# Attention weights transposed by DMA instead of TensorE, and MLP chunks as one stream of alternating first and last products

## The chip, the cores and the metric

The kernel runs on one core of one Trainium2 chip. Its time is the device time of that core in microseconds, from the first instruction to the last. Three runs of the kernel before took 1746.2, 1747.33 and 1747.04 us; the median is 1747.04.

A core has five engines that run side by side, each executing its own queue of instructions in order, with semaphores between them: TensorE (PE, matrix products; results go to PSUM, here in banks of 512 float32 per partition), VectorE (DVE), ScalarE (ACT), GpSimd (POOL) and SyncE (SP), which here issues the DMAs. Tiles have 128 partitions.

## What is computed

Top-32 attention over 8 batches of 8 heads, 576 queries and keys of 64 elements, and then a feed-forward block (MLP) over the 4608 rows of 512 that come out of it, with a hidden width of 2048:

```python
scores = scale * np.matmul(q, k.transpose(0, 1, 3, 2))
kth = np.partition(scores, -32, axis=-1)[..., -32:-31]
scores = np.where(scores >= kth, scores, -1e9)
scores = scores - np.max(scores, axis=-1, keepdims=True)
attn = np.exp(scores)
attn = attn / (np.sum(attn, axis=-1, keepdims=True) + 1e-09)
x = np.matmul(attn, v)                    # then (B,H,S,D) -> (B*S, H*D)

h = x @ w_in                              # 4608x512 @ 512x2048
g = np.where(h >= 1, h, np.where(h <= -1, 0.0, (h + 1) ** 2 / 4))
out = g @ w_out                           # 4608x2048 @ 2048x512
```

q, k and v are float32. The two weight matrices come as 64-bit floats, and the kernel makes 32-bit floats of them, from the two 32-bit words of each.

## The kernel before

A step of attention takes one tile of 128 queries and two heads; there are 144. Tokens are laid out so that 512 of the 576 keys form four blocks of 128 (`main`), and the last 64 of the two heads share a fifth (`tail`). In a step TensorE makes the scores, ScalarE evicts them from PSUM and takes exponentials, VectorE finds the 32nd largest score, GpSimd divides by the sum, TensorE transposes the attention weights (with the keys on the partitions, as the product with the values needs them), ScalarE evicts the transposed blocks, and TensorE multiplies them with the values.

`paired` is true for the run that is timed: VectorE looks for the largest among 288 pairwise maxima and corrects by the pairwise minima. A second run without that shortcut follows only if a flag says that the shortcut, or a very small weight, was not covered; the flag is also what `inspect_piece` and `judge` are for.

Weights are converted in 64 pieces of 128x256, first all of w_in, then all of w_out, by two instructions of ScalarE, one or two of VectorE and one or two of GpSimd each, during the first 12 steps:

```python
pieces_of_weights = [(w_in[:, kk, c:c + WC], moe_w_in[kk * P:(kk + 1) * P, c:c + WC])
                     for c in range(0, DFF, WC) for kk in range(NK)]
pieces_of_weights += [(w_out[:, f, c:c + WC], moe_w_out[f * P:(f + 1) * P, c:c + WC])
                      for f in range(NF) for c in range(0, DM, WC)]
```

Scores, the top-32 search (VectorE throughout), the softmax weights, their transposing and the product with the values:

```python
def scores(st):
    t, hp, kT, qT = st["t"], st["hp"], st["keys"]["kT"], st["qT"]
    st["s"] = s = att.tile([P, 2, S], F32, name="s", bufs=3)
    for hf in range(2):
        sp = [ps.tile([P, SH], F32, name="sp", tag="a", bufs=4) for _ in range(2)]
        c0, c1 = hf * SH, (hf + 1) * SH
        for i in range(2):
            for j in ([i] if t < NT else [0, 1]):
                d = slice(j * D, (j + 1) * D)
                g = hp if t < NT else hp + i
                o = sp[i] if t < NT else sp[i][j * TL:(j + 1) * TL]
                for a0, a1, k0 in pieces(i, j, c0, c1):
                    nc.tensor.matmul(o[:, a0 - c0:a1 - c0], qT[d, g, :], kT[d, g, k0:k0 + a1 - a0],
                                     start=True, stop=True)
        for i in range(2):
            nc.scalar.activation(s[:, i, c0:c1], sp[i], AF.Copy, scale=SCALE)
# ...
def pairs(st):
    s = st["s"]
    st["more"] = more = att.tile([P, 2, SH], F32, name="more")
    nc.vector.tensor_tensor(out=more, in0=s[:, :, 0:SH], in1=s[:, :, SH:S], op=ALU.max)
def weights(st, after):
    s, m = st["s"], st["m"]
    tops = att.tile([P, 2, TOP_K + 8], F32, name="tops", bufs=3)
    st["e"] = e = att.tile([P, 2, S], F32, name="e")
    nmax = att.tile([P, 2], F32, name="nmax")
    kth = att.tile([P, 2, 8], F32, name="kth", bufs=3)
    if paired:
        src = rest = less = st["more"]
    else:
        src, rest = s, att.tile([P, 2, S], F32, name="rest", bufs=1)
    for r in range(0, TOP_K, 8):
        for i in range(2):
            nc.vector.max(out=tops[:, i, r:r + 8], in_=src[:, i, :])
        if r == 0:
            nc.scalar.activation(nmax, tops[:, :, 0], AF.Copy, scale=-1.0)
            for i in range(2):
                nc.scalar.activation(e[:, i, :], s[:, i, :], AF.Exp, bias=nmax[:, i:i + 1])
                if i == 0:
                    yield
        if r + 8 < TOP_K:
            for i in range(2):
                nc.vector.match_replace(out=rest[:, i, :], in_to_replace=tops[:, i, r:r + 8],
                                        in_values=src[:, i, :], imm_value=LOWEST)
            src = rest
        yield
    if paired:
        nc.vector.tensor_tensor(out=less, in0=s[:, :, 0:SH], in1=s[:, :, SH:S], op=ALU.min)
        seconds = att.tile([P, 2, 8], F32, name="seconds")
        for i in range(2):
            nc.vector.max(out=seconds[:, i, :], in_=less[:, i, :])
        nc.vector.tensor_tensor(out=tops[:, :, TOP_K:TOP_K + 8], in0=tops[:, :, TOP_K - 2:TOP_K - 10:-1],
                                in1=seconds, op=ALU.min)
        for i in range(2):
            nc.vector.max(out=kth[:, i, :], in_=tops[:, i, TOP_K - 1:TOP_K + 8])
        last = kth[:, :, 0]
    else:
        last = tops[:, :, TOP_K - 1]
    if paired and after is not None:
        pairs(after)
    z = att.tile([P, 2], F32, name="z")
    for i in range(2):
        nc.vector.scalar_tensor_tensor(out=e[:, i, :], in0=s[:, i, :], scalar=last[:, i:i + 1],
                                       in1=e[:, i, :], op0=ALU.is_ge, op1=ALU.mult,
                                       accum_out=z[:, i:i + 1])
    yield
    rz = att.tile([P, 2], F32, name="rz")
    nc.vector.tensor_scalar(z, z, 1e-9, None, ALU.add)
    nc.vector.reciprocal(rz, z)
    if st["by_tensor"]:
        st["rz"] = diag = att.tile([P, 2, P], F32, name="diag", bufs=1)
        for i in range(2):
            nc.scalar.activation(diag[:, i, :], ident, AF.Copy, scale=rz[:, i:i + 1])
    else:
        for i in range(2):
            nc.gpsimd.tensor_scalar(e[:, i, :], e[:, i, :], rz[:, i:i + 1], 1.0, ALU.mult, ALU.mult)
# ...
def transpose_w(st):
    w = st["e"]
    st["wT"] = wT = att.tile([P, 2, NT, P], F32, name="wT", bufs=1)
    st["wTt"] = wTt = att.tile([P, P], F32, name="wTt", bufs=1)
    for i in range(2):
        pt = ps.tile([P, NT, P], F32, name="pw", tag="a", bufs=4)
        for c in range(NT):
            w_in_place = w[:, i, main(i)][:, c * P:(c + 1) * P]
            if st["by_tensor"]:
                nc.tensor.matmul(pt[:, c, :], w_in_place, st["rz"][:, i, :], start=True, stop=True)
            else:
                nc.tensor.transpose(pt[:, c, :], w_in_place, ident)
        nc.scalar.copy(wT[:, i], pt)
    pt = ps.tile([P, P], F32, name="pwt", tag="a", bufs=4)
    if st["by_tensor"]:
        for i in range(2):
            nc.tensor.matmul(pt[i * TL:(i + 1) * TL, :], w[:, i, tail(i)], st["rz"][:, i, :],
                             start=True, stop=True)
    else:
        nc.tensor.transpose(pt, w.rearrange("p i n -> p (i n)")[:, SM:SM + P], ident)
    nc.scalar.copy(wTt, pt)
# ...
def values(st):
    t, hp, v_in, v_tl = st["t"], st["hp"], st["keys"]["v"], st["keys"]["v_tl"]
    wT, wTt = st["wT"], st["wTt"]
    po = ps.tile([P, P], F32, name="po", tag="ph", bufs=3)
    if t < NT:
        for c in range(NT + 1):
            for j in range(2):
                h = 2 * hp + j
                nc.tensor.matmul(po[j * D:(j + 1) * D], v_in[:, h, c, :] if c < NT else v_tl[0][:, h, :],
                                 wT[:, j, c, :] if c < NT else wTt, start=(c == 0), stop=(c == NT))
```

`by_tensor` steps (those during the conversion) fold the division into the transposing, by multiplying with a diagonal matrix of 1/sum; the others have it done by GpSimd (`L325`) and transpose with the identity.

An MLP chunk is one tile of 128 tokens or two. For each of 16 blocks f of the hidden width, `hidden` makes the first product into PSUM tile `ph` and the activation as min(relu(h/2 + 1/2), 1)^2 + relu(h - 1) on ScalarE and GpSimd; `final` adds to `py`. The first products of a chunk all come before the last products, and all 16 `g` are kept:

```python
def hidden(f, c0, c1):
    ph = ps.tile([P, CW], F32, name="ph", tag="ph", bufs=3)[:, 0:c1 - c0]
    for kk in range(NK):
        nc.tensor.matmul(ph, w_in[:, kk, f * P:(f + 1) * P], xT[:, kk, c0:c1],
                         start=(kk == 0), stop=(kk == NK - 1))
    r = pool.tile([P, CW], F32, name="r", bufs=2)[:, 0:c1 - c0]
    nc.scalar.activation(r, ph, AF.Relu, bias=half, scale=0.5)
    if f not in gs:
        gs[f] = pool.tile([P, CW], F32, name="g", bufs=NF)
    g = gs[f][:, c0:c1]
    if last:
        nc.vector.tensor_scalar(g, ph, -1.0, 0.0, ALU.add, ALU.max)
        nc.scalar.activation(r, r, AF.Square)
        nc.vector.scalar_tensor_tensor(out=g, in0=r, scalar=1.0, in1=g, op0=ALU.min, op1=ALU.add)
        return
    if converted < n_pieces and f % 2:
        nc.scalar.activation(r, r, AF.Square)
        nc.scalar.activation(g, ph, AF.Relu, bias=minus, scale=1.0)
        nc.gpsimd.tensor_scalar(r, r, 1.0, 0.0, ALU.min, ALU.max)
    else:
        nc.scalar.activation(g, ph, AF.Relu, bias=minus, scale=1.0)
        nc.gpsimd.tensor_scalar(r, r, 1.0, 0.0, ALU.min, ALU.max)
        nc.gpsimd.tensor_tensor(out=r, in0=r, in1=r, op=ALU.mult)
    nc.gpsimd.tensor_tensor(out=g, in0=r, in1=g, op=ALU.add)
def final(i, f0, f1):
    if f0 == 0:
        pys[i] = ps.tile([P, DM], F32, name="py", tag="py")
    py = pys[i]
    for f in range(f0, f1):
        nc.tensor.matmul(py, gs[f][:, i * P:(i + 1) * P], w_out[:, f, :],
                         start=(f == 0), stop=(f == NF - 1))
    if f1 == NF:
        y = pool.tile([P, DM], F32, name="y", bufs=1)
        nc.scalar.copy(y, py)
```

The chunks, and the loop that puts their products between the parts of the attention steps (`advance` does so by a model of TensorE's and VectorE's time; each step has 7 slots):

```python
rounds, chunks = [], []
for b in range(0, B, 2):
    a, c, tl = [(b, t) for t in range(NT)], [(b + 1, t) for t in range(NT)], (b, NT)
    if b + 2 < B:
        rounds += a + [tl] + c + [(b + 1, NT)]
        chunks += [a[0:2], a[2:4], c[0:2], c[2:4], [tl]]
    else:
        rounds += a + [tl, (b + 1, NT)] + c
        chunks += [a[0:2], a[2:4], [tl], c[0:2], c[2:3], c[3:4]]
# ...
for m in range(n + 2):
    # ... values and scores(m + 2) here, once the conversion is over
    top_k = weights(state[m], state[m + 1] if m + 1 < n else None)
    # ...
    for slot in range(SLOTS):
        # ... next(top_k), some parts in each slot; convert(now) while pieces are left
        if slot == 1 + (not early) and 1 <= m <= n:
            transpose_w(state[m - 1])
        # ... while converting: values in slot 2, scores(m + 2) in slot 4; queries and keys of later steps
        advance(min(share, EARLY_SHARE if early else share) / SLOTS if m < n else 0.0, now, not early)
```

## Time and profile before

| | |
|---|---|
| time, median of three | 1747.04 us |
| span of the profiled run | 1744.5 us |
| mean granted TensorE clock | 0.982 |
| attention steps | 144 |
| DMA traffic over the span | 74.6 MB, 43 GB/s |

In the profile, `L258` is a line of the kernel, and `sp<-kT,qT` names the tile written and the tiles read. "x1056" counts instruction records; a float32 product that is not a transposing one has two. "busy" is the time in which at least one instruction of a group ran, "mean ns" the length of one record; records of TensorE overlap, so the mean times the count is more than the busy time. PEld are TensorE's weight loads. A wait "A <- B" names the instruction that waited and the one whose end it waited for, with its total in us, how often, and the longest. A table of stages gives, for each stretch of the span, the busy time of PE, PEld, DVE, ACT and POOL in us, each with its number of records, then the granted clock, the DMA engines' busy share and GB/s.

### The profile page before, as it was taken

What the parts mean: (1) busy time and instruction counts of PE and PEld (TensorE: products, weight loads), DVE (VectorE), ACT (ScalarE), POOL (GpSimd) and SP (SyncE); (2) the same over time, 40 slices, a digit from 0 to 9 for tenths busy, and PEclk for the clock granted to TensorE, in tenths of its full rate; (3) what the DMA queues carried; (4) which work ended last, traced back from release to release, by engine and by line L of the source; (5) the groups of instructions that cost most, each with busy time, mean ns of one, the idle gap of its engine ahead of it and who ended that gap; (6) DMA issues with size and microseconds to landing.
All of it is one profiled execution on the core that took longest, in us unless ns stands there. A gap on an engine that the chain in (4) does not pass through costs nothing.

```text
span 1744.5 us, 33535 instructions
## 1 busy us (share of the span) xinstructions
PE 1639.4 (94%) x10665; PEld 1151.5 (66%) x10665; DVE 1537.0 (88%) x4875; ACT 1083.2 (62%) x2942; POOL 946.9 (54%) x1668
## 2 busy tenths in 40 slices
PE   5588989999999999999999999999999999999998
PEld 4476575667766757476756767567667666666665
DVE  7999979888899999999987999999997998899752
ACT  6688575676667857576655647556555555466452
POOL 5689183665544817264646645436365554555550
PEclk7799999999999999999999999999999999999999
DMA  8333112111121112111200101000010000000000
GB/s 253 116 98 97 46 30 65 44 43 41 42 63 52 44 49 65 46 49 41 62 13 22 25 22 44 17 24 17 23 39 19 19 10 14 13 7 7 7 7 15
DMA packets 116668, 74.63 MB, mean 43 GB/s; under 512 B 87296, under 2 KB 95488, under 8 KB 116480
## 3 DMA queue, kind: packets, MB, share of 16 engines
q1 hardware_dynamic: 116480, 72.37, 14.5%
q8 instruction: 87, 1.43, 0.3%
q14 instruction: 101, 0.83, 0.2%
HBM read 62.91 MB, written 9.44 MB: 41 GB/s over the span
## 4 chain that ended last, share of the span: by engine, by line
PE 65%; DVE 14%; POOL 11%; ACT 6%; issue 3%; DMA 0%; POOLq 0%; DVEq 0%; SPq 0%; ACTq 0%
PE py L422 25%; PE ph L394 18%; PE sp L258 7%; PE po L364 7%; PE pw L344 5%; DVE tops L283 4%; DVE more L292 3%; POOL g L415 3%; POOL r L414 3%; DVE e L312 3%; POOL e L325 2%; POOL r L413 2%; ACT s L261 1%; DVE seconds L300 1%; ACT r L398 1%
## 5 line engine op out<-in xcount | busy, mean ns | idle before, releaser
L394 PE MATMUL ph<-xT,w_in 128*128 128x128 f32 (+1 forms) x3200 | 558.0, 326 | 14.4 <-ACT g L412 13.2
L422 PE MATMUL py<-w_out,g 128*128 128x512 f32 x1152 | 530.9, 600 | 2.0 <-ACT y L426 2.0
L394 PEld LDWEIGHTS ph<-xT,w_in 128*128 128x128 f32 x3200 | 472.3, 192 | 87.9 <-ACT g L412 26.0
L325 POOL TENSOR_SCALAR e<-e,rz 128x576 f32<-128x576 f32 x264 | 195.0, 750 | 520.2 <-DVE rz L318 488.8
L283 DVE MAX8 tops<-more 128x8 f32<-128x288 f32 x1152 | 465.4, 445 | 0.0
L292 DVE MATCH_REPLACE8 more<-tops,more 128x288 f32<-128x288 f32 x864 | 375.6, 442 | 0.0
L422 PEld LDWEIGHTS py<-w_out,g 128*128 128x128 f32 x1152 | 205.2, 190 | 224.1 <-issue 215.8
L312 DVE SCALAR_TENSOR_TENSOR e<-s,kth,e 128x576 f32<-128x576 f32 x288 | 245.7, 881 | 116.6 <-ACT e L287 116.3
L398 ACT ACTIVATE r<-ph,half 128x128 f32<-128x128 f32 (+1 forms) x400 | 166.5, 416 | 216.8 <-POOL g L415 156.7
L415 POOL TENSOR_TENSOR g<-r,g 128x128 f32<-128x128 f32 (+1 forms) x384 | 255.9, 666 | 30.2
L413 POOL TENSOR_SCALAR r<-r 128x128 f32<-128x128 f32 (+1 forms) x368 | 173.2, 471 | 132.0 <-ACT r L398 131.7
L414 POOL TENSOR_TENSOR r<-r 128x128 f32<-128x128 f32 (+1 forms) x368 | 213.9, 581 | 30.7
L261 ACT ACTIVATE s<-sp 128x288 f32<-128x288 f32 x576 | 195.2, 421 | 56.8 <-PE sp L258 36.8
L287 ACT ACTIVATE e<-s,nmax 128x576 f32<-128x576 f32 x288 | 213.4, 770 | 7.7
L364 PEld LDWEIGHTS po<-wT,v_in 128*64 128x64 f32 x2048 | 111.8, 137 | 87.9 <-issue 53.2
L258 PE MATMUL sp<-kT,qT 64*128 64x288 f32 x1024 | 163.9, 437 | 4.2 <-ACT kT L218 2.3
L364 PE MATMUL po<-wT,v_in 128*64 128x128 f32 x2048 | 145.5, 280 | 18.7 <-ACT g L412 11.3
L345 ACT COPY wT<-pw 128x512 f32<-128x512 f32 x288 | 154.0, 589 | 13.1 <-PE pw L344 10.6
L344 PEld LDWEIGHTS pw<-ident,e 128*128 128x128 f32 x1056 | 122.2, 142 | 60.0 <-issue 24.4
L344 PE MATMUL pw<-ident,e 128*128 128x128 f32 x1056 | 141.0, 276 | 16.2 <-ACT s L261 10.4
L377 ACT COPY xT<-po 128x128 f32<-128x128 f32 x128 | 34.1, 266 | 195.8 <-PE po L364 195.5
L412 ACT ACTIVATE g<-ph,minus 128x128 f32<-128x128 f32 (+1 forms) x368 | 153.6, 417 | 0.0
(91 smaller groups left out, 1595.1 us busy)
## 6 DMA issues: line engine op xcount, KB each, us to landing
raw<-in_moe_w_out_dram SPq DMA_DIRECT2D x64, 256.0 KB, 2.6
raw<-in_moe_w_in_dram SPq DMA_DIRECT2D x36, 256.0 KB, 2.7
k_in<-in_k_dram SPq DMA_DIRECT2D x64, 128.0 KB, 2.9
q_in<-in_q_dram SPq DMA_DIRECT2D x32, 256.0 KB, 3.1
v_in<-in_v_dram SPq DMA_DIRECT2D x8, 1024.0 KB, 5.8
out_dram<-y SPq DMA_DIRECT2D x32, 256.0 KB, 2.3
kT<-in_moe_w_in_dram SPq DMA_DIRECT2D x16, 256.0 KB, 4.0
v_in<-in_moe_w_in_dram SPq DMA_DIRECT2D x12, 256.0 KB, 4.5
```

Source lines behind the costliest of these rows:

```text
L258: nc.tensor.matmul(o[:, a0 - c0:a1 - c0], qT[d, g, :], kT[d, g, k0:k0 + a1 - a0], start=True, stop=True)
L283: nc.vector.max(out=tops[:, i, r:r + 8], in_=src[:, i, :])
L287: nc.scalar.activation(e[:, i, :], s[:, i, :], AF.Exp, bias=nmax[:, i:i + 1])
L292: nc.vector.match_replace(out=rest[:, i, :], in_to_replace=tops[:, i, r:r + 8], in_values=src[:, i, :], imm_value=LOWEST)
L312: nc.vector.scalar_tensor_tensor(out=e[:, i, :], in0=s[:, i, :], scalar=last[:, i:i + 1], in1=e[:, i, :], op0=ALU.is_ge, op1=ALU.mult, acc ...
L325: nc.gpsimd.tensor_scalar(e[:, i, :], e[:, i, :], rz[:, i:i + 1], 1.0, ALU.mult, ALU.mult)
L344: nc.tensor.transpose(pt[:, c, :], w_in_place, ident)
L364: nc.tensor.matmul(po[j * D:(j + 1) * D], v_in[:, h, c, :] if c < NT else v_tl[0][:, h, :], wT[:, j, c, :] if c < NT else wTt, start=(c == ...
L394: nc.tensor.matmul(ph, w_in[:, kk, f * P:(f + 1) * P], xT[:, kk, c0:c1], start=(kk == 0), stop=(kk == NK - 1))
L414: nc.gpsimd.tensor_tensor(out=r, in0=r, in1=r, op=ALU.mult)
L415: nc.gpsimd.tensor_tensor(out=g, in0=r, in1=g, op=ALU.add)
L422: nc.tensor.matmul(py, gs[f][:, i * P:(i + 1) * P], w_out[:, f, :], start=(f == 0), stop=(f == NF - 1))
```

## The change

Three parts, meant to take work from TensorE and to keep its queue supplied evenly.

1. Attention weights are transposed by DMA. In the 130 steps after the conversion, except the last two, `transpose_w` gives way to `move_w`: ScalarE copies each weight's low and high 16-bit half into two separate runs (the transposing DMA here moves 2-byte elements), one DMA writes them to a DRAM buffer, and a second, transposing DMA brings them back as `wT`. Reading both halves side by side makes the 32-bit words whole again. The product with the values comes a step later than before, so that the two DMAs have time.
2. Each MLP chunk is one stream: first product of block x, then the last product of block x - 4 (`LAG`), so that 8 `g` are kept instead of 16. Weight pieces are converted in the order in which this stream needs them. Chunks of the first two batches are single tiles throughout, and the last batch's too.
3. Scores go into PSUM tiles of two banks, two halves of heads each, and are evicted by one instruction instead of two. The pool for scores and transposes has two such tiles instead of four of one bank; `ph` has 2 buffers instead of 3, `py` 2 instead of 1.

The first maximum and the exponentials of step m + 1 (`first_top`) are also moved into step m, ahead of its last round of maxima. Memory for the conversion (`words`) is given back when it is over, and used by the later stage (`late`).

```diff
+    pieces_of_weights = []
+    for c in range(0, DFF, WC):
+        pieces_of_weights += [(w_in[:, kk, c:c + WC], moe_w_in[kk * P:(kk + 1) * P, c:c + WC]) for kk in range(NK)]
+        pieces_of_weights += [(w_out[:, f, x:x + WC], moe_w_out[f * P:(f + 1) * P, x:x + WC])
+                              for f in range(c // P, (c + WC) // P) for x in range(0, DM, WC)]
+    n_in, n_out = WC // P, DM // WC
+    def needed(f, second):
+        return (f // n_in) * (NK + n_in * n_out) + NK + (n_out * (f % n_in + 1) if second else 0)
 # ...
-                sp = [ps.tile([P, SH], F32, name="sp", tag="a", bufs=4) for _ in range(2)]
+                sp = ps.tile([P, 2, BANK], F32, name="sp", tag="a", bufs=2)
 # ...
-                    nc.scalar.activation(s[:, i, c0:c1], sp[i], AF.Copy, scale=SCALE)
+                nc.scalar.activation(s[:, :, c0:c1], sp[:, :, 0:SH], AF.Copy, scale=SCALE)
 # ...
+        def first_top(st):
+            s = st["s"]
+            if paired:
+                pairs(st)
+            st["tops"] = tops = att.tile([P, 2, TOP_K + 8], F32, name="tops", bufs=3)
+            st["e"] = e = att.tile([P, 2, S], F32, name="e", bufs=3)
+            nmax = att.tile([P, 2], F32, name="nmax")
+            for i in range(2):
+                nc.vector.max(out=tops[:, i, 0:8], in_=(st["more"] if paired else s)[:, i, :])
+            nc.scalar.activation(nmax, tops[:, :, 0], AF.Copy, scale=-1.0)
+            for i in range(2):
+                nc.scalar.activation(e[:, i, :], s[:, i, :], AF.Exp, bias=nmax[:, i:i + 1])
+                yield
 # ...
+            for r in range(8, TOP_K, 8):
+                for i in range(2):
+                    nc.vector.match_replace(out=rest[:, i, :], in_to_replace=tops[:, i, r - 8:r],
+                                            in_values=src[:, i, :], imm_value=LOWEST)
+                src = rest
+                if r == 8:
+                    yield
+                if r + 8 == TOP_K:
+                    yield
+                    yield from first_top(after) if after is not None else (None, None)
                 for i in range(2):
                     nc.vector.max(out=tops[:, i, r:r + 8], in_=src[:, i, :])
+            st["wT"] = wT = (late or words).tile([P, BLOCKS, P], F32, name="wT", bufs=2 if late else 1)
+            pt = ps.tile([P, 2, NT, P], F32, name="pw", tag="a", bufs=2)
 # ...
+        def move_w(st):
+            st["wT"] = wT = late.tile([P, BLOCKS, P], F32, name="wT", bufs=2)
+            halves = late.tile([P, 2, 2 * S], U16, name="halves")
+            for i in range(2):
+                nc.scalar.copy(halves[:, :, i * S:(i + 1) * S], st["e"][:, i, :].bitcast(U16).rearrange("p (k t) -> p t k", t=2))
+            rows = dram.tile([P, 2, 2 * S], U16, name="rows")
+            nc.sync.dma_start(out=rows, in_=halves)
+            nc.sync.dma_start_transpose(wT.bitcast(U16), rows.rearrange("p t k -> (p t) k"))
+        def block(i, c):
+            return i * (NT + 1) + c if c < NT else NT
 # ...
+            def final(f):
+                for i in range(len(tiles)):
+                    if f == 0:
+                        pys[i] = ps.tile([P, DM], F32, name="py", tag="py", bufs=2)
+                    nc.tensor.matmul(pys[i], gs[f][:, i * P:(i + 1) * P], w_out[:, f, :],
                                      start=(f == 0), stop=(f == NF - 1))
 # ...
+            n_tiles, work = len(tiles), []
+            for x in range(NF + LAG):
+                if x < NF:
+                    work.append((NK * n_tiles, needed(x, False), partial(hidden, x, 0, n_tiles * P)))
+                if x >= LAG:
+                    work.append((n_tiles * DM // P, needed(x - LAG, True), partial(final, x - LAG)))
+            return work
 # ...
-                chunks += [a[0:2], a[2:4], c[0:2], c[2:4], [tl]]
+                chunks += [a[0:2], a[2:4], c[0:2], c[2:4], [tl]] if b else [[x] for x in a + c + [tl]]
             else:
                 rounds += a + [tl, (b + 1, NT)] + c
-                chunks += [a[0:2], a[2:4], [tl], c[0:2], c[2:3], c[3:4]]
+                chunks += [a[0:2], a[2:4], [tl]] + [[x] for x in c]
 # ...
+                state[m]["by_tensor"] = early or m >= n - 2
 # ...
+                if slot == 1 and 1 <= m <= n and state[m - 1]["by_tensor"]:
                     pe_time = max(pe_time, done[m - 1] + 2.0) + 1.0
                     transpose_w(state[m - 1])
-                    transposed = pe_time
+                    ready_at[m - 1] = pe_time + 1.8
+                if slot == 2 and 1 <= m <= n and not state[m - 1]["by_tensor"]:
+                    move_w(state[m - 1])
+                    ready_at[m - 1] = done[m - 1] + 14.0
 # ...
-                if slot == 4 and early:
+                if slot == 4:
                     begin_at(m + 2)
-                if slot == (5 if early else 4):
+                if slot == 5 and not early:
+                    values_until(m - 1)
```

## The prediction

> **What bounds the kernel now.** I read the page's first two parts, then the table of stages, the times at which one small VectorE instruction recurs, the waits, and last the groups of the operations that the change touches. Busy shares first:
>
> ```profile
> PE 1639.4 (94%) x10665; PEld 1151.5 (66%) x10665; DVE 1537.0 (88%) x4875; ACT 1083.2 (62%) x2942; POOL 946.9 (54%) x1668
> ```
>
> Two engines are nearly full. The stages (PE, weight loads, VectorE, ScalarE, GpSimd busy in each, then clock, DMA share, GB/s) show who leads where:
>
> ```profile
> 12.00:200.00 188.00, 141.27 (x965) 105.77 (x967) 182.93 (x560) 142.61 (x392) 130.43 (x206) 0.87 0.42 125
> 200.00:550.00 350.00, 327.74 (x2432) 237.52 (x2430) 300.61 (x973) 234.90 (x703) 199.85 (x423) 1.00 0.16 47
> 550.00:1690.00 1140.00, 1114.27 (x6982) 770.23 (x6978) 1037.48 (x3295) 684.52 (x1792) 606.62 (x1011) 1.00 0.10 28
> 1690.00:1745.00 55.00, 47.66 (x256) 30.85 (x254) 12.39 (x42) 16.70 (x47) 6.04 (x13) 0.97 0.04 13
> ```
>
> Up to 200 us VectorE is 97% busy: it leads, because it also converts weights. From then on TensorE is 94 to 98% busy and VectorE 86 to 91%: TensorE leads, and the last 53 us are TensorE alone. One attention step (two heads, 128 queries) ends in a reciprocal on VectorE; there are 144. A stretch in the timeline:
>
> ```profile
> 1210.61 0.17 DVE L318 RECIPROCAL rz<-z 128x2 f32<-128x2 f32 x1
> 1220.79 0.17 DVE L318 RECIPROCAL rz<-z 128x2 f32<-128x2 f32 x1
> 1230.96 0.17 DVE L318 RECIPROCAL rz<-z 128x2 f32<-128x2 f32 x1
> 1241.76 0.17 DVE L318 RECIPROCAL rz<-z 128x2 f32<-128x2 f32 x1
> 1252.29 0.17 DVE L318 RECIPROCAL rz<-z 128x2 f32<-128x2 f32 x1
> 1264.04 0.17 DVE L318 RECIPROCAL rz<-z 128x2 f32<-128x2 f32 x1
> 1276.26 0.17 DVE L318 RECIPROCAL rz<-z 128x2 f32<-128x2 f32 x1
> ```
>
> 10.2 us is VectorE's own work in a step; it is the shortest gap anywhere after the conversions. The longer gaps are steps in which VectorE waited, or was slowed. The 12th reciprocal, the last of the converting steps, is at 174.0 us and the 144th at 1691.9, so the 132 steps between take 11.5 us each, 1.3 above VectorE's own 10.2. What VectorE waits for:
>
> ```profile
> DVE e L312 <- ACT e L287: 116.3, 80, 6.3
> ```
>
> It waits for the exponentials, which wait for scores that TensorE, behind with its queue, delivered late.
>
> **What the Trainium skill says.** "Perfetto Trace Analysis", Identifying the Most-Contended Engine, says that matmul busy time is no measure of how near TensorE is to its peak and that the share of weight loads is a better one. Here that share is 66%, so "94%" does not mean a full array; but TensorE executes its queue in order and has few idle gaps, so for this schedule removing instructions is what gives it time. "SBUF — State Buffer", Who interferes with whom, says that a VectorE instruction with two SBUF inputs contends with a GpSimd one that reads SBUF. The trace agrees: the maximum of two halves (L269) takes 0.74 us with GpSimd idle and 1.05 us at 567.8 us beside GpSimd's MLP operations. "DMA: Bandwidth & Descriptors", Latency and other measured facts, gives 261 GB/s for a transposing DMA in one kernel; "VectorE: DVE Perf Modes", The three transpose paths, gives 1.3 us for one 128x128 tile of 2-byte elements. No run here has a transposing DMA yet; the two figures make two very different forecasts, used below.
>
> **TensorE's part.** The groups to be removed or replaced:
>
> ```profile
> L344 PE MATMUL pw<-ident,e 128*128 128x128 f32 x1056 | 141.0, 276 | 16.2 <-ACT s L261 10.4
> L352 PE MATMUL pwt<-ident,e 128*128 128x128 f32 x132 | 36.3, 275 | 0.0
> L345 ACT COPY wT<-pw 128x512 f32<-128x512 f32 x288 | 154.0, 589 | 13.1 <-PE pw L344 10.6
> ```
>
> All 132 steps of transposes by identity go: 141.0 + 36.3 = 177 us, 1.34 us a step. Two of these steps, the last ones, are done in the form with the diagonal matrix instead (from the groups: 33.1 + 6.1 us for 12 steps, 3.3 us each): +7. The chunk list also changes: single-tile chunks go from 14 to 16, double ones from 11 to 10. A single one is 128 records of 230.6/1792 = 0.129 us, a double one 128 of 327.4/1408 = 0.233: +33 and -30. TensorE: 1639 - 177 + 7 + 33 - 30 = 1472 us. By 200 us it had done 150, and the tail (below) holds about 60, so 1262 us lie in the 130 or so steps between, 9.7 us a step. At the 94 to 98% that TensorE reaches today this is 9.9 to 10.4 us: slightly below what VectorE needs. So TensorE stops leading, without much room.
>
> **VectorE's part.** It executes the same instructions; the first maximum and the exponentials of the next step only move ahead into the current one, which removes the cause of the 116 us wait if the scores are there. What remains is 10.2 us plus the interference. In the eight-step cycles where VectorE never waits today (550 to 700 us has no wait at all) the gaps run 11.4, 11.4, 11.4, 10.2 (four times) and about 10.8: mean 10.7. GpSimd's total stays (+12 us for the extra narrow tiles), only more evenly spread, so I take 10.7 us a step.
>
> **ScalarE's part.** Removed: 130 x (2 x 0.589 + 0.288) = 191 us of evictions of transposed weights. The 576 score evictions become 288 twice as large; copies of 128, 256 and 512 elements take 0.288, 0.382 and 0.589 us, so about 0.19 us is fixed and 0.79 ns is paid per element, and 288 fixed parts are 54 us. Added: 260 copies that split e into low and high 16-bit halves, 1152 elements each, estimated at 0.19 + 1152 x 0.00079 = 1.10 us: 286. Sum 1083 - 191 - 54 + 286 = 1124 us, 68% of the new span. Beside other work.
>
> **DMA's part.** Each of 130 steps writes 576 KB to DRAM and reads it back transposed. Loads of 256 KB land in 2.6 us and of 1024 KB in 5.8 us, so about 1.5 us is fixed and the rate 246 GB/s; the write then takes 3.9 us. The transposed read, at the skill's 261 GB/s, is estimated at 2.3 + 1.5 = 3.8 us. From the reciprocal: GpSimd's scaling 1.5, halves 2.2, perhaps 2 of queueing, 3.9, 3.8: some 13 us. The products with the values come one step and five sevenths later, 18.3 us. It fits, with 5 us to spare. Traffic grows by 153 MB to about 140 GB/s; the first 50 us moved 245.
>
> **Streams and banks.** Alternating first and last products halves the rate at which TensorE throws results at ScalarE and GpSimd, so the waits of ScalarE for GpSimd (L398 on L415, 157 us) and of TensorE for evictions should shrink. The conversion order changes no instruction count; up to 174 us VectorE leads anyway. I give both nothing beyond letting TensorE keep its 94 to 98%.
>
> **The tail.** In the changed program's order, behind the last step's transposes lie 10 value products, three last products, and two whole single-tile chunks, where today one is left. From the timeline one chunk is 14.45 + 13.90 = 28.4 us. Scaling, transposing, evicting: 5.6; values and copy 1.8; three products 2.6; 56.7 for the chunks; result copy and store 2.9: 70 us, against 52.6 now.
>
> **Sum.** 174 + 132 x 10.7 + 70 = 174 + 1412 + 70 = 1656 us. I predict 1655, a ratio of 0.947.
>
> **Rivals.**
> (1) The transposing DMA is slow. A step's read is 18 tiles; at 1.3 us one after another, 24 us. The DMA queue would be busy for 28 us a step, and the kernel would take over twice as long. Even 10 us of transposing gives 14 us a step and about 2090 us. For it: nothing has been measured here. Against it: the schedule leaves just the 14 to 18 us of the quicker estimate.
> (2) VectorE and TensorE, both nearly full, make each other wait: scores now have 0.9 of a step between issue and first use instead of 1.8. At 11.2 us a step it is 174 + 1478 + 70 = 1722 us, within 2%.
> (3) Even spreading removes the interference and VectorE runs at 10.2 us: 174 + 1346 + 70 = 1590 us.
>
> **Range and chances.** Between (3) and (2) I take 1600 to 1712. Faster by over 2% means below 1712: 0.86. Rival (2) mostly lands within 2%: 0.07. Slower needs rival (1): 0.07.
>
> **What would show it.** Right: reciprocals 10.5 to 10.9 us apart after 180 us, VectorE over 94% busy between, TensorE near 1472 us busy and about 90%, VectorE's wait for the exponentials below 30 us, the two DMAs landing in 3 to 5 us each, and some 70 us after the last reciprocal. Wrong: waits of the value products for the transposing DMA, or of VectorE for scores; halves on ScalarE well above 1.1 us; steps of 11.2 us or more.

## The result, and the profile after

The changed kernel takes 1684.5 us, median of four runs (1680.3 to 1685.4), against 1746.6 (1743.3 to 1747.3) for the kernel before in the same series: a ratio of 0.9643, 95% interval 0.9623 to 0.9664. The profiled execution spans 1683.5 us, at a mean granted clock of 0.952 (before: 1744.5 us, 0.982).

First part of the page, the changed kernel:

```profile
PE 1549.2 (92%) x9645; PEld 1050.8 (62%) x9645; DVE 1550.5 (92%) x4875; ACT 1188.2 (71%) x2552; POOL 974.8 (58%) x1720
```

TensorE lost 90 us and a tenth of its records. Two engines are now equally full. The stages of the changed kernel (PE, weight loads, VectorE, ScalarE, GpSimd, then clock, DMA share, GB/s):

```profile
12.00:200.00 188.00, 131.52 (x866) 98.49 (x865) 179.83 (x539) 129.56 (x323) 116.54 (x178) 0.80 0.43 121
200.00:550.00 350.00, 327.24 (x2298) 224.60 (x2297) 331.24 (x1046) 265.79 (x598) 236.79 (x466) 0.98 0.55 146
550.00:1620.00 1070.00, 1025.31 (x6125) 679.97 (x6126) 1026.58 (x3252) 766.53 (x1559) 599.72 (x1013) 0.97 0.52 141
1620.00:1690.00 70.00, 56.96 (x321) 40.87 (x319) 9.33 (x32) 22.66 (x67) 18.11 (x48) 0.96 0.04 13
```

In the long stage both TensorE and VectorE are at 96%, where before it was 98 and 91. The DMA engines went from a tenth to half busy. The reciprocals, read as in the prediction: the 12th is at 179.6 us, the 144th at 1607.5, the 132 steps between take 10.82 us on average (shortest 10.36, but for the last step, which prepares no next one and takes 8.98; median 10.69), and 76.0 us follow the last.

The waits of the changed kernel that answer to "VectorE waits for exponentials: 116.3 us":

```profile
DVE g L427 <- ACT r L423: 46.1, 16, 33.2
DVE more L279 <- ACT s L271: 10.7, 12, 2.1
PE po L389 <- DMA wT<-rows: 13.9, 7, 3.6
PE ph L419 <- ACT g L431: 18.6, 25, 1.8
```

The wait for the exponentials is gone from the list. The first line belongs to the MLP's last chunk, which costs no step. VectorE waits for scores for 10.7 us in all, and the products with the values wait for the transposing DMA only seven times.

The two DMAs of a step (KB and median us from issue to landing; the second has no size in the record), and how the queue that issues them looks in the timeline around 1400 us:

```profile
rows<-halves SPq DMA_DIRECT2D x130, 576.0 KB, 2.8
wT<-rows SPq DMA_TRANSPOSE x130, 4.8
```

```profile
1395.97 0.34 SPq L374 DMA_DIRECT2D rows<-halves  x1
1398.91 2.63 SPq L375 DMA_TRANSPOSE wT<-rows  x1
```

The step whose reciprocal is at 1392.18 writes from 1395.97 and reads back from 1398.91, so its transposed weights are there at 1398.91 + 4.8 = 1403.7, 11.5 us after the reciprocal. That is one of the quickest steps: over all 130 the median is 15.5 us, from 10.6 to 23.8.

### The profile page after: what moved, and what is told of

Same layout as the page of the kernel before. It is cut to its first block, busy times and chain, and to the rows that moved or that the text cites. A ratio compares the mean times of both kernels' runs of the same rounds, so it can differ in the third digit from the quotient of the medians.

```text
span 1683.5 us, 30910 instructions
## 1 busy us (share of the span) xinstructions
PE 1549.2 (92%) x9645; PEld 1050.8 (62%) x9645; DVE 1550.5 (92%) x4875; ACT 1188.2 (71%) x2552; POOL 974.8 (58%) x1720
## 4 chain that ended last, share of the span: by engine, by line
DVE 51%; PE 33%; ACT 7%; issue 3%; POOL 3%; DMA 2%; SPq 1%; DVEq 0%; POOLq 0%; ACTq 0%
PE ph L419 13%; DVE more L306 12%; PE py L444 12%; DVE tops L315 10%; DVE e L330 8%; DVE more L317 4%; DVE seconds L320 4%; DVE tops L290 4%; DVE more L279 4%; PE po L389 3%; PE sp L269 3%; ACT halves L372 2%; ACT e L293 1%; DVE z L335 1%; DVE kth L324 1%
## 5 line engine op out<-in xcount | busy, mean ns | idle before, releaser
L419 PEld LDWEIGHTS ph<-xT,w_in 128*128 128x128 f32 x3328 | 505.1, 195 | 199.0 <-issue 88.5
L419 PE MATMUL ph<-xT,w_in 128*128 128x128 f32 (+1 forms) x3328 | 594.1, 326 | 32.8 <-ACT g L431 18.6
L444 PE MATMUL py<-w_out,g 128*128 128x512 f32 x1152 | 564.3, 605 | 2.0 <-POOL w_out L136 1.8
L315 DVE MAX8 tops<-more 128x8 f32<-128x288 f32 x864 | 348.9, 445 | 0.0
L343 POOL TENSOR_SCALAR e<-e,rz 128x576 f32<-128x576 f32 x260 | 211.9, 825 | 205.2 <-DVE rz L336 205.2
L372 ACT COPY halves<-e 128x1152 uint16<-128x1152 uint16 x260 | 286.9, 1156 | 14.7 <-POOL e L343 14.0
L271 ACT ACTIVATE s<-sp 128x576 f32<-128x576 f32 x288 | 170.0, 642 | 6.6 <-PE sp L269 6.4
L389 PEld LDWEIGHTS po<-wT,v_in 128*64 128x64 f32 x2048 | 115.5, 141 | 80.7 <-issue 18.3
L269 PEld LDWEIGHTS sp<-kT,qT 64*128 64x128 f32 x1024 | 91.8, 193 | 84.6 <-issue 40.6
L320 DVE MAX8 seconds<-more 128x8 f32<-128x288 f32 x288 | 118.3, 452 | 13.9
L317 DVE TENSOR_TENSOR more<-s 128x576 f32<-128x576 f32 x144 | 122.4, 850 | 4.9
```

What stands on the lines that cost most here:

```text
L372: nc.scalar.copy(halves[:, :, i * S:(i + 1) * S], st["e"][:, i, :].bitcast(U16).rearrange("p (k t) -> p t k", t=2))
L444: nc.tensor.matmul(pys[i], gs[f][:, i * P:(i + 1) * P], w_out[:, f, :], start=(f == 0), stop=(f == NF - 1))
```

## The experiments

In each, "the step" is the mean of the 132 steps, "the tail" the time after the last reciprocal; times are medians, and a ratio is to the kernel before. All edits are to the changed kernel unless another is named.

**1. The transposes back on TensorE.** Only the way of transposing differs; schedule, streams, banks and early exponentials stay.

```diff
-                        nc.tensor.matmul(pt[:, i, c, :], ..., st["rz"][:, i, :], start=True, stop=True)
+                        if st["by_tensor"]: # as above, else:
+                            nc.tensor.transpose(pt[:, i, c, :], w[:, i, main(i)][:, c * P:(c + 1) * P], ident)
 # ...
-                    move_w(state[m - 1])
+                    transpose_w(state[m - 1])
```

> The changed kernel with the 130 late steps' transposes given back to TensorE (by identity, in the same place of the order, values at the same later place; no halves, no DRAM round trip). If relieving TensorE is what brought the gain, its 172 us come back (about 1.3 us a step), TensorE leads again, steps rise from 10.8 to 11.5 us or more and the time goes to 1740 to 1790 us. If the gain came from the streams or from the moved exponentials, it stays below 1705 us, and VectorE still never waits for exponentials.

Measured: 1771.5 us, ratio 1.0155 (1.0138 to 1.0172); step 11.46, tail 77.3. Page and wait of this version:

```profile
PE 1655.7 (94%) x10815; PEld 1156.1 (65%) x10815; DVE 1572.9 (89%) x4875; ACT 1079.7 (61%) x2682; POOL 980.9 (55%) x1720
```

```profile
DVE more L279 <- ACT s L271: 67.6, 55, 3.1
```

TensorE is as full as before the change (94%), the step as long (11.50 before), and VectorE, which waited for exponentials then, waits for the scores that lead to them: with TensorE this full, moving the exponentials ahead did not shorten a step. Without the DMA transposes the change loses 25 us, as much as the tail grows (77.3 against 52.6). So the DMA transposes bring 1771.5 - 1684.5 = 87 us, and of these 132 x (11.46 - 10.82) = 84 lie in the steps. This holds beside the other parts of the change; what the DMA transposes would bring to the kernel before, alone, no run shows.

**2. A longer lag.** The last product trails the first by eight blocks instead of four, with nine `g` instead of eight; nine blocks with ten `g` did not fit into SBUF.

```diff
-    LAG = 4
+    LAG = 8
-                gs[f] = pool.tile([P, CW], F32, name="g", bufs=2 * LAG)
+                gs[f] = pool.tile([P, CW], F32, name="g", bufs=LAG + 1)
```

> Last products follow the first ones of their block at a distance of 8 instead of 4 (9 buffers of g instead of 8): each chunk begins with 8 first products in a row and ends with 8 last ones. If the evenness of the stream matters little once VectorE leads: within 8 us of the changed kernel, 1676 to 1692. If bursts bring back waits of TensorE for evictions or slow VectorE through GpSimd: 1700 us or more.

Measured: 1723.7 us, ratio 0.9877 (0.9861 to 0.9894); step 11.06, tail 80.0. Waits of this version:

```profile
PE ph L419 <- ACT g L431: 48.4, 48, 2.7
DVE more L279 <- ACT s L271: 39.3, 19, 3.4
```

39 us slower. With long runs of first products TensorE waits for their two PSUM tiles to be emptied, 48 us instead of 19, and VectorE's scores come late behind that queue. Even alternation matters.

**3. One eviction of a two-bank score tile split into two.**

```diff
-                nc.scalar.activation(s[:, :, c0:c1], sp[:, :, 0:SH], AF.Copy, scale=SCALE)
+                for i in range(2):
+                    nc.scalar.activation(s[:, i, c0:c1], sp[:, i, 0:SH], AF.Copy, scale=SCALE)
```

> Scores evicted by two instructions per two-bank tile instead of one. ScalarE gets 288 instructions and about 54 us more (1188 to about 1240 us). Theory: it lies beside VectorE, time within 6 us of the changed kernel. Rival: ScalarE's queue is what delays TensorE and VectorE (it is 71 to 80 percent busy in the middle), time 15 us or more above it.

Measured: 1685.3 us, ratio 0.9664 (0.9648 to 0.968), its interval overlapping that of the change; step 10.81. ScalarE was busy for 1204.1 us, 16 more and not 54. The fixed part that two instructions pay hardly shows, because neighbours on ScalarE overlap: the 576 evictions of this version, 411 ns each, were busy for 187.0 us together, the 288 of the changed kernel, 642 ns each, for 170.0. The single eviction is worth nothing that these runs can resolve.

**4. GpSimd's part of the MLP left out.** This version does not compute the minimum, the square and the sum: `g` is only relu(h - 1). It shows what GpSimd's work costs the others.

```diff
-                if converted < n_pieces and f % 2:
-                    nc.scalar.activation(r, r, AF.Square)
-                    nc.gpsimd.tensor_scalar(r, r, 1.0, 0.0, ALU.min, ALU.max)
-                else:
-                    nc.gpsimd.tensor_scalar(r, r, 1.0, 0.0, ALU.min, ALU.max)
-                    nc.gpsimd.tensor_tensor(out=r, in0=r, in1=r, op=ALU.mult)
-                nc.gpsimd.tensor_tensor(out=g, in0=r, in1=g, op=ALU.add)
```

> The changed kernel without GpSimd's three operations on each block of the MLP (minimum, square, sum): g is only relu(h - 1), so part of the activation is left out. If GpSimd's reads are what lengthens VectorE's steps above their shortest 10.37 us, the mean of the last 132 steps falls from 10.82 to 10.55 or less and the time to 1635 to 1660. If TensorE's lag lengthens them, the mean stays at 10.75 or more.

Measured: 1649.0 us, ratio 0.9447 (0.9431 to 0.9462); step 10.56, median 10.37, that is, the shortest step of the changed kernel (10.36). VectorE's groups, in the changed kernel and then in this version (busy us, mean ns of one):

```profile
L315 DVE MAX8 tops<-more 128x8 f32<-128x288 f32 x864 | 348.9, 445 | 0.0
L330 DVE SCALAR_TENSOR_TENSOR e<-s,kth,e 128x576 f32<-128x576 f32 x288 | 242.0, 877 | 0.5
L317 DVE TENSOR_TENSOR more<-s 128x576 f32<-128x576 f32 x144 | 122.4, 850 | 4.9
```

```profile
L315 DVE MAX8 tops<-more 128x8 f32<-128x288 f32 x864 | 348.9, 445 | 0.0
L330 DVE SCALAR_TENSOR_TENSOR e<-s,kth,e 128x576 f32<-128x576 f32 x288 | 224.4, 817 | 0.4
L317 DVE TENSOR_TENSOR more<-s 128x576 f32<-128x576 f32 x144 | 111.3, 773 | 4.9
```

The maxima, with one input, take the same 445 ns; the two operations with two inputs take 60 and 77 ns less. That agrees with the Trainium skill, "SBUF — State Buffer", Who interferes with whom: a VectorE instruction with two SBUF inputs contends with a GpSimd one that reads SBUF, one with at most one does not, but for the modes that use both ports for it. GpSimd's MLP work costs 132 x (10.82 - 10.56) = 34 us in the steps and 4 before the twelfth. That is what is left after a quicker VectorE has waited longer for scores, 23.1 us instead of 10.7:

```profile
DVE more L279 <- ACT s L271: 23.1, 23, 2.3
```

**5. VectorE's order.** In a step of the changed kernel several instructions wait for the one just before them. This version puts independent ones in between. The edit is given in short, by the order of the work:

```diff
         # ... after the last match_replace of the step, "after" is the next step:
-        pairs(after); max(after, 0); max(after, 1); exponentials(after)
-        max24(0); max24(1); less; seconds(0); seconds(1); tops; kth(0); kth(1); e(0); e(1)
+        max24(0); max24(1); pairs(after); less; max(after, 0); seconds(0); seconds(1); max(after, 1)
+        exponentials(after)   # ScalarE
+        tops; kth(0); kth(1); e(0); e(1)
```

> VectorE's order inside a step changed so that no instruction directly follows the one that it depends on where the next step's maximum or pairs can stand between; same instructions. In the changed kernel the shortest step is 10.37 us against 10.18 before, since the pairs no longer stand between kth and the product that needs it. Theory: VectorE leads, so its own step falls to 9.9 to 10.1 us and the time by 25 to 55 us, to 1630 to 1660. Rival (TensorE is just as full): less than 12 us.

Measured: 1665.1 us, ratio 0.9536 (0.952 to 0.9552), 19 us less than the changed kernel and between the two expectations. The shortest step fell from 10.36 to 9.77, the mean only from 10.82 to 10.69. VectorE's timeline in the changed kernel, then in this version, same part of a step (start, duration):

```profile
1406.74 0.75 DVE L279 TENSOR_TENSOR more<-s 128x576 f32<-128x576 f32 x1
1407.52 0.82 DVE L290 MAX8 tops<-more 128x8 f32<-128x288 f32 x2
1408.26 0.80 DVE L315 MAX8 tops<-more 128x8 f32<-128x288 f32 x2
```

```profile
1398.77 0.74 DVE L279 TENSOR_TENSOR more<-s 128x576 f32<-128x576 f32 x1
1399.43 0.75 DVE L332 TENSOR_TENSOR more<-s 128x576 f32<-128x576 f32 x1
1400.10 0.45 DVE L334 MAX8 tops<-more 128x8 f32<-128x288 f32 x1
```

From one start to the next, an operation of 0.75 us takes 0.78 where its result is used at once (1406.74 to 1407.52) and 0.66 where it isn't (1398.77 to 1399.43): these independent neighbours overlap by 0.1 us, the dependent ones don't overlap. Four such places (at one of them the next instruction writes over what the one before reads) make up 0.55 of the 0.6 us of the shortest step. The mean got little of it, since other costs took its place, waits first:

```profile
DVE more L279 <- ACT s L271: 37.9, 27, 3.1
```

38 us of waiting for scores instead of 11, which is 0.2 us a step; and each of the two `scalar_tensor_tensor` of a step took 939 ns instead of 877, 0.12 us a step, for which meeting GpSimd's work more often is the likely reason, not tested. By the starts of VectorE's instructions, a mean step of the changed kernel is its shortest 10.36, plus 0.09 of waiting for scores and 0.36 in which instructions take longer than in the shortest step; here it is 9.77, plus 0.31 and 0.60. So of the 0.59 gained, 0.22 came back as waits and 0.24 as longer instructions.

**6. Squares on ScalarE, on top of 5.** Half of the squares go from GpSimd to ScalarE in the first version, all that follow the conversion in the second.

```diff
-                if converted < n_pieces and f % 2:
+                if f % 2:                              # second: if f % 2 or converted >= n_pieces:
                     nc.scalar.activation(r, r, AF.Square)
```

> The reordered VectorE version (1665 us), with the square of every other hidden block on ScalarE instead of GpSimd during the whole run. About 190 GpSimd products of 0.56 us go (107 us), and ScalarE gains as many squares of some 0.35 us (66 us: 1188 to about 1254, 75%). Leaving all of GpSimd's MLP work out (some 650 us) gave 35 us. If the interference goes by GpSimd's busy time, a sixth of it gives 6 us: 1659. If ScalarE's queue is what makes the others wait (it evicts the scores and feeds the hidden blocks), it costs more than it gives: 1668 to 1680.

> As the run before, but with all squares on ScalarE once the conversion is over: about 380 of GpSimd's products go (213 us), ScalarE gains some 133 us (to about 1320, 79%). If the interference goes by GpSimd's busy time: 12 us less than the reordered version, 1653. If ScalarE's queue is what makes the others wait: 1675 or more.

Measured: 1667.1 and 1668.8 us, ratios 0.9547 (0.9527 to 0.9567) and 0.9557 (0.9534 to 0.958), neither told apart from version 5. GpSimd went from 997 us busy to 889 and 791, VectorE from 1531 to 1523 and 1516: it was indeed disturbed less. The wait for scores, 37.9 us in version 5, took that back, first version and second:

```profile
DVE more L279 <- ACT s L271: 47.2, 34, 3.2
```

```profile
DVE more L279 <- ACT s L271: 56.6, 43, 3.4
```

The first came out just below the range expected for a loss by ScalarE's queue, the second between its two expectations: the gain is there, and later evictions cancel it. On average ScalarE began the second eviction of a step's scores 1.67 us after their last product had ended in version 5, and 1.83 and 1.95 us here.

**7. Single-tile chunks throughout**, alone and on top of 5.

```diff
-                chunks += [a[0:2], a[2:4], c[0:2], c[2:4], [tl]] if b else [[x] for x in a + c + [tl]]
+                chunks += [[x] for x in a + c + [tl]]
 # ...
-                chunks += [a[0:2], a[2:4], [tl]] + [[x] for x in c]
+                chunks += [[x] for x in a + [tl] + c]
```

> All chunks single tiles (36 instead of 16 single and 10 double). TensorE's time is the same by the records (0.226 us per 256 columns in two narrow ones, 0.233 in a wide one). Theory: in the changed kernel TensorE runs out of MLP work near 520, 720 and 1120 us because a double chunk comes late, and is two chunks behind at the end; with single ones by the order of instructions 37 us of MLP are left behind the last step instead of 60, the tail falls from 76 to about 53 us, and the time to 1655 to 1670. Rival: ScalarE (+86 us) and GpSimd (+117 us), with their smaller instructions, slow the steps by 0.15 us or more and the time stays above 1675.

> Single chunks together with the VectorE order of the third run, which alone gave 1665 us. If the two act on different stretches (steps and tail), their gains add up: 1665 less 15 to 28 us, 1637 to 1650. If TensorE is the common limit: above 1655.

Measured: 1729.7 and 1715.7 us, ratios 0.9905 (0.9889 to 0.9922) and 0.9824 (0.9808 to 0.9841). The tail fell to 54.2 and 59.9 us, as expected, but the step rose to 11.36 and 11.19, so that the rival was right both times. Waits of the first:

```profile
DVE more L279 <- ACT s L271: 74.3, 53, 4.4
PE ph L419 <- ACT g L431: 43.0, 54, 2.0
```

Narrow chunks give ScalarE and GpSimd more instructions for the same work (GpSimd was busy for 1134 us instead of 975, ScalarE for 1240 instead of 1188), and TensorE waits longer for its hidden tiles. That the first leads to the second, and both to the late scores, is the likely order of causes; the runs don't separate them.

**8. Double-tile chunks where the change made them single.** The first two batches' list of chunks as before the change: on top of 5, alone, and, on top of 5, the last batch's as well. (The kernel before had this list, but made the first products of its first four chunks tile by tile; here they are double as well.)

```diff
-                chunks += [a[0:2], a[2:4], c[0:2], c[2:4], [tl]] if b else [[x] for x in a + c + [tl]]
+                chunks += [a[0:2], a[2:4], c[0:2], c[2:4], [tl]]
 # third version, also:
-                chunks += [a[0:2], a[2:4], [tl]] + [[x] for x in c]
+                chunks += [a[0:2], a[2:4], [tl], c[0:2], c[2:3], c[3:4]]
```

> The reordered VectorE version (1665 us), with the chunks of the first two batches as double tiles again, as the kernel before has them, instead of nine single ones. Narrow chunks cost ScalarE and GpSimd a fixed part per instruction and TensorE 0.129 against 0.233 / 2 = 0.117 us per tile and record: 8 tiles x 128 x 0.0125 us = 13 us of TensorE. If, as the run with single chunks throughout showed, narrow chunks are what makes steps long, the steps between 200 and 550 us shorten by about 0.4 us each (some 30 steps: 12 us) and the time is 1650 to 1656. If double chunks supply their products too late for the first steps after the conversion (a chunk can start only when all its attention steps are done), TensorE stands idle there and the time is 1670 or more.

> The changed kernel with only the chunks of the first two batches as double tiles again, VectorE's order left as the change has it. If the narrow chunks cost by themselves (ScalarE's and GpSimd's fixed parts, TensorE's 13 us) and add to the order's cost, it gains the same 18 us as between the two reordered versions: 1664 to 1668. If the two overlap (VectorE must be quick for the gain to show), it gains under 10: 1675 or more.

> The reordered version with double tiles in the first two batches (1646.5 us), and the last batch's chunks too as in the kernel before: two of its single chunks become one double one. TensorE gains 128 x (2 x 0.129 - 0.233) = 3 us. If narrow chunks are what costs, some of the last steps shorten: 1640 to 1645. If single chunks there serve the even supply near the end (the step-long parts left over grow with the size of a chunk), it is 1648 to 1655.

Measured: with the order, 1646.5 us, ratio 0.9438 (0.9418 to 0.9457); alone, 1671.9, ratio 0.9575 (0.9559 to 0.9591); with the last batch too, 1644.8, ratio 0.9416 (0.94 to 0.9431). The stage from 200 to 300 us of version 5, then of the first version here:

```profile
200.00:300.00 100.00, 96.50 (x696) 66.92 (x696) 92.88 (x303) 75.55 (x177) 74.61 (x146) 1.00 0.55 144
```

```profile
200.00:300.00 100.00, 93.25 (x561) 60.87 (x562) 99.00 (x317) 70.72 (x139) 60.20 (x84) 0.97 0.58 155
```

With double tiles VectorE is 99% busy there and no longer held up; the 16 steps between the 20th and the 36th reciprocal take 10.32 us instead of 11.24. Over the whole kernel the wait for scores fell from 38 us to 18. Alone the double tiles gain 12.6 us, between the two expectations; with the quicker order they gain 18.5. The last batch's chunks made no difference that can be told. The best version, 1644.8 us, is 2.4% below the changed kernel: it keeps the DMA transposes and the streams, reorders VectorE and has no more single chunks than the old list.

## Why the prediction was right, and where its sizes were off

The prediction was 1655 us, range 1600 to 1712, faster by over 2% at 0.86; it came to 1684.5. Its sum, term by term:

| term | predicted | measured | adds |
|---|---|---|---|
| 12th reciprocal | 174 | 179.6 | +6 |
| 132 steps | 10.7 each, 1412 | 10.82 each, 1427.8 | +16 |
| tail | 70 | 76.0 | +6 |
| sum | 1656 | 1683.5 | +28 |

**TensorE stops leading: right, shown by 1 above.** Its busy time was mis-sized: 1549 us instead of 1472. Most of the 77 us are in the term for the transposes, 177 us or 1.34 a step, which adds the busy times of two groups whose records overlap with each other and with their neighbours. One step of the kernel before:

```profile
1048.85 1.04 PE L344 MATMUL pw<-ident,e 128*128 128x128 f32 x8
1049.72 0.27 PE L352 MATMUL pwt<-ident,e 128*128 128x128 f32 x1
1049.83 1.45 PE L422 MATMUL py<-w_out,g 128*128 128x512 f32 x3
```

From the first transpose to the next product it is 0.98 us, also the median of the 132 steps: some 130 us. Giving the transposes back (1 above) added only 1655.7 - 1549.2 = 106 us of busy time. So 47 to 71 of the 77 us are this term; for the rest a lower clock (0.952 against 0.982) is a candidate, not separated. At 96% in the long stage TensorE came out level with VectorE, and not "slightly below". Rival (2), the two making each other wait, was little at work in the changed kernel, 0.09 us a step, but stands close: in experiments 5 and 6 much of what VectorE was relieved of came back as waiting for scores. The 77 us are 0.6 us in each of some 130 steps, most of the room that the prediction saw between TensorE's 9.7 and the step of 10.7, so that VectorE still led was in part luck.

**VectorE's 10.2 us of its own: failed by 0.2.** The prediction said that VectorE "executes the same instructions", only earlier. Their order counts. Before the change the pairs of the next step stood between `kth` and the operations that use it and filled that gap; the change puts each pair maximum right before its own first use. The shortest step became 10.36. What was added, 0.5 us of interference, was about right: 10.82 - 10.36 = 0.46, of which waits for scores are 10.7 / 132 = 0.08. Leaving out GpSimd's MLP work took off 0.26 (4 above), although the waits grew by (23.1 - 10.7) / 132 = 0.09; without that it would be 0.35, nearly all of the rest.

**Rival (3), even spreading removes the interference: wrong.** Experiment 4 had to leave GpSimd's work out to remove it.

**ScalarE: the halves were right, the sum 64 us short.** Its group in the changed kernel:

```profile
L372 ACT COPY halves<-e 128x1152 uint16<-128x1152 uint16 x260 | 286.9, 1156 | 14.7 <-POOL e L343 14.0
```

1.156 us against 1.10. The saving of 54 us by larger evictions was mis-sized (16 by experiment 3); with 38 of the 64 us that is the larger part. It cost no time by itself.

**DMA: rival (1) was wrong, the hidden chain right.** The write lands in 2.8 us (3.9 predicted) and the transposed read in 4.8 (the estimate from the rate of 261 GB/s in the Trainium skill, "DMA: Bandwidth & Descriptors", Latency and other measured facts, was 3.8): 15.5 us from the reciprocal in all at the median, where 13 were predicted and 18.3 there were. Most of what was longer lies ahead of the write, which is issued 7.3 us after the reciprocal (median), where scaling, halves and queueing were put at 5.7. 14 us of waiting in seven places is what is left of it.

**The streams: not sized.** "I give both nothing beyond letting TensorE keep its 94 to 98%" took the alternation for a detail. Half of it, a lag of eight, costs 39 us (2 above), so in this kernel it is no detail; what it gained over the old arrangement no run shows. The chunk list was counted as TensorE time alone. Double chunks in the first two batches, first products included, are worth 12.6 us (8 above): a gain left out rather than a cost added, since the kernel before made those first products singly too.

**The tail: right, 6 us short.** The end of the MLP in TensorE's timeline, changed kernel:

```profile
1620.07 4.93 PE L419 MATMUL ph<-xT,w_in 128*128 128x128 f32 x40
...
1644.10 4.46 PE L444 MATMUL py<-w_out,g 128*128 128x512 f32 x10
1648.40 5.00 PE L419 MATMUL ph<-xT,w_in 128*128 128x128 f32 x40
...
1672.50 4.46 PE L444 MATMUL py<-w_out,g 128*128 128x512 f32 x10
```

Two whole chunks, 1672.50 + 4.46 - 1620.07 = 56.9 us, against 56.7 predicted. What is ahead of them took 12.6 us instead of 10, and what follows 6.5 instead of 2.9.

**The twelfth reciprocal**, 6 us late, was taken to be unchanged. Without GpSimd's MLP work it is at 175.9, with double tiles alone at 176.9; but versions that convert the weights as the changed kernel does, with single chunks, have it anywhere between 177.1 (6 above, first version) and 179.6, so no cause is shown.

Left open: what the DMA transposes bring without the streams and the early exponentials, and whether the longer VectorE instructions of experiment 5 come from GpSimd.

## What to carry to other kernels

Where two engines are both above 90%, expect little from relieving one: after the 87 us of the DMA transposes, 0.6 us taken from VectorE's shortest step brought 0.13 on average, and 0.2 with double chunks (10.73 to 10.53, both versions with double tiles). What came back was waiting for the other engine and longer instructions (5 above). Take what an engine spends on a group of overlapping instructions from their starts, not from the sum of busy times (0.98 us a step, not 1.34). Count instructions per unit of work on the evicting engines when choosing chunk sizes, and keep the in-order queue of TensorE alternating between work that needs evictions and work that doesn't. In a full VectorE queue, put an independent instruction between one and the next that uses its result.

## What the runs showed of the hardware

- A DMA that transposes 576 KB of 2-byte elements from DRAM into SBUF landed 4.8 us after its issue (median of 130; 4.4 to 8.2), and held the issuing queue for 2.6 us (median; 2.2 to 5.3), where the plain DMA of the same size held it for 0.34.
- A VectorE instruction of 0.75 us whose result was used by the next took 0.78 us from start to start, one followed by an independent instruction 0.66.
- Of the changed kernel's 50 us windows between 200 and 1650 us, the three in which TensorE was busy least (77 to 81%) had the lowest granted clock (0.76 to 0.90, the others 0.93 or more). It is no rule: from 100 to 150 us the kernel before had 85% and a clock of 1.00. What lowers the clock isn't shown. The lowest of the three, and a full window:

```profile
700.00:750.00 50.00, 39.10 (x210) 23.88 (x209) 48.49 (x159) 34.98 (x67) 12.87 (x23) 0.76 0.60 163
1300.00:1350.00 50.00, 49.89 (x322) 34.52 (x321) 48.46 (x154) 42.31 (x93) 37.20 (x69) 1.00 0.51 140
```

- Single and double evictions of a two-bank PSUM tile cost ScalarE 1204 and 1188 us in the whole kernel: 288 further instructions for 16 us.
